# Second products in pairs of steps, absolute values on ScalarE, and one convolution moved to TensorE

## Chip, cores and metric

One NeuronCore of one Trainium2 chip runs the whole program. The metric is the device time in microseconds (us) from the start to the end of the program. PE is TensorE (PEld its weight loads), DVE is VectorE, ACT is ScalarE, POOL is GpSimd, SP is SyncE, which issues most transfers.

## The reference

```python
# x: (4, 4096, 192), weight: (8, 7); both MLPs: 192 -> 2048 -> 192 on 16384 tokens
w = softmax(weight)                       # 7 taps for each of 8 groups of 24 channels
x = causal_conv(x, w)                     # each channel with the 7 taps of its group
h = x @ moe_w_in;  x = (h * np.cos(h)) @ moe_w_out
h = x @ moe2_w_in
g = np.where(h > 0.0, h, np.exp(np.minimum(h, 0.0)) - 1.0)
out = g @ moe2_w_out
```

Weights of the MLPs are drawn by the reference's own functions; the kernel reads them as pairs of 32-bit words (the 64-bit floats of the inputs) and rebuilds each value in float32. That rebuilding is called decoding here.

## The kernel before

Tokens lie along the free dimension in 32 blocks of 512. Channels lie on partitions: 128 lower channels, and 64 upper ones, of which two blocks share a 128-partition tile. The hidden dimension of 2048 is cut into 16 chunks of 128. A step is two such chunks of one block, so a block takes 8 steps in each MLP. Blocks go in groups of four: a group runs MLP 1 (m = 1) and then MLP 2 (m = 2), so there are 512 steps. Steps 0 to 31 are MLP 1 of blocks 0 to 3; blocks 0 and 1 take turns by half blocks of four steps.

To keep float32 accuracy, every operand is a high part and a low part, and each product is three products. In step s, TensorE does the first products of step s (`products_A`, 18 matmuls of 64 rows, two at a time beside each other in the two halves of the array) and the second products of step s-3 (`LAG` = 3). While weights are being decoded, only two PSUM banks are free for the second products, so these are 10 matmuls over all 128 rows (`whole_B`, L567). This holds for the blocks that begin before decoding is over, steps 0 to 31; from step 32 on, the second products are 64-row matmuls woven into the first ones (L583).

The order on every engine is written out by hand: what `step` emits first runs first on that engine. A step emits its products, and then for each of its two chunks t = 2s and 2s+1: `emit_act1(t)` (ACT, L608), `emit_mid(t)` (DVE, L617), `emit_act2(t-1)` (ACT, L623), `emit_g(t-1)` (DVE, L631), one decode advance if it is due, `emit_hi(t-2)` (ACT, L637), `emit_lo(t-2)` (POOL, L644). So `emit_g` of the second chunk of a step stands in the next step, behind `emit_act1` and `emit_mid` of that next step's first chunk. The first products land in a ring of four PSUM banks (`ring_bank`, u0 to u3), two for each step; a bank is free when `emit_g` of its chunk has read it. High and low parts of g rotate through six buffers each.

A decoded piece passes ACT (L195, and L197 for the absolute value in two of three pieces), DVE (L199, L201 for the absolute value in the third piece, L202, L203), POOL (L205), ACT (the high part) and POOL (the low part). Thirty pieces are decoded in all.

`opening` is called after each of the first steps and carries the work of the first blocks. Lower channels of blocks 0 to 2 are convolved by TensorE with diagonal tap matrices (`conv_by_products`, L403, 7 products in float32, two matmul records each). The shared upper channels of blocks 2 and 3 are convolved by VectorE (`conv_taps`, L374 and L376), one tap after each of steps 5 to 11, and split into parts (`split_pair`, L437 and L439) when block 2 is split. `spare` is a scratch tile in the place that MLP 2's weights take later.

Of the kernel before, what the change touches and what calls it, by code (L numbers as in the profile page):

```python
# [18 lines left out]
P = 128  # L19
N = 512  # L20
# [12 lines left out]
def conv_then_two_mlps(ctx, tc, x, weight, w_in1, w_out1, w_in2, w_out2, out):  # L33
# [139 lines left out]
        zp = zt.tile([P, 2, N], F32R, tag=f"zp{b % ZN}", name="z")  # L173
        return zp[:, 0], zp[:, 1], zt.tile([P, N], F32R, tag=f"zc{b % ZN}", name="z")

    turn, scalar = deque(("", "e1", "")), deque((0, 1, 1))

    def decode(m, load, n):

        raw, use = raw_tile(n)
        load(raw)
        yield
        lo, hi = raw[..., 0], raw[..., 1]
        brink.reverse()
        t = brink[0][:, 0:n]
        turn.rotate(-1)  # L190
        w = (op if turn[0] else stage).tile([P, N], F32, tag=turn[0] or "w", name="w")[:, 0:n]
        bits = w.bitcast(I32)
        scalar.rotate(-1)
        size = w if scalar[0] else t
        nc.scalar.activation(out=t, in_=lo.bitcast(U32), func=AF.Copy, scale=2.0 ** -51, bias=2.0)  # L195
        if size is w:
            nc.scalar.activation(out=w, in_=f32(hi), func=AF.Abs)  # L197
        yield
        nc.vector.scalar_tensor_tensor(out=lo, in0=hi, scalar=SIGN, in1=t.bitcast(I32), op0=ALU.bitwise_and, op1=ALU.bitwise_or)  # L199
        if size is t:  # L200
            nc.vector.tensor_scalar(out=t.bitcast(I32), in0=hi, scalar1=~SIGN, scalar2=0, op0=ALU.bitwise_and, op1=ALU.bitwise_or)  # L201
        nc.vector.tensor_scalar(out=t, in0=size, scalar1=2.0 ** -15, scalar2=2.0 ** 17 - 2.0 ** 13, op0=ALU.max, op1=ALU.min)  # L202
        nc.vector.tensor_scalar(out=bits, in0=t.bitcast(I32), scalar1=3, scalar2=0, op0=ALU.logical_shift_left, op1=ALU.bitwise_or)  # L203
        yield
        nc.gpsimd.tensor_tensor(out=bits, in0=bits, in1=lo, op=ALU.add)  # L205
        taken.difference_update(use)
        yield w
# [91 lines left out]
    rows = rows[:, 0:at].rearrange("p (k d) -> p k d", d=D)  # L299
    xc0, xc1, xa2, xc2 = (spare[:, c * NX:(c + 1) * NX] for c in range(4))  # L300
    fold_rows = spare[:, 4 * NX:4 * NX + P]
    turn_rows = op.tile([P, N], F32R, tag="e0", name="turn")[:, 0:P]

    def load_rows():
# [90 lines left out]
            nc.tensor.matmul(y[:, 0:P], lhsT=ident, rhs=ident, start=True, stop=True)  # L395
        return y

    def conv_by_products(b, o):


        xT = xTs.pop(("a", b))
        for k in range(K):
            nc.tensor.matmul(o, lhsT=taps[:, k], rhs=xT[:, k * Q:k * Q + N], start=k == 0, stop=k == K - 1)  # L403
            if k == K - 1:
                ys["a", b] = o
            yield

    def conv_packed(b):
# [165 lines left out]
    def ends_here(m, b, j):  # L574
        return j == NP - 1 or split_up(m, b) and j == NP // 2 - 1

    def side_by_side(*streams):

        for pr in zip_longest(*streams):
            for product in pr:  # L580
                if product:
                    o, lhsT, rhs, first, final = product
                    nc.tensor.matmul(o, lhsT=lhsT, rhs=rhs, start=first, stop=final)  # L583

    def products(s):
        now, then = 0 <= s < total, 0 <= s - LAG < total
        if then and steps[s - LAG][2] == 0 and not late:
            whole.add(steps[s - LAG][:2])
        if not then or steps[s - LAG][:2] in whole:
            if now:  # L590
                side_by_side(products_A(2 * s), products_A(2 * s + 1))
            if then:
                whole_B(s - LAG)
        elif not now:
            side_by_side(products_B(s - LAG, 0), products_B(s - LAG, 1))
        else:
            streams = products_B(s - LAG, 0), products_B(s - LAG, 1)
            side_by_side(chain(products_A(2 * s), streams[0]), chain(streams[1], products_A(2 * s + 1)))
        if then:
            for i in (0, 1):  # L600
                del gs[f"{s - LAG} {i}"]

    def emit_act1(s):
        m = steps[s // 2][0]
# [233 lines left out]
    def need(m, at, *kinds):  # L838
        while any(ready.get((k, m), 0) < at for k in kinds):
            assert loaded or any(stages.values())  # L840
            advance()
# [32 lines left out]
    def step(s):  # L874
        now = 0 <= s < total
        present[0] = s
        if now:
            m, b, j = steps[s]
            need(m, j + 1, "o", "c")
        finish = iter(())  # L880
        if 0 <= s - LAG < total:
            m, b, j = steps[s - LAG]
            need(m, 2 * j + 2, "oh", "os")
        products(s)
        ends = 0 <= s - LAG < total and ends_here(*steps[s - LAG])
        if ends:
            assert not lazy
            finish = evac(*steps[s - LAG])
        if s in begin_at:
            m, b = begin_at[s]  # L890
            chores.append(begin_split(b) if m == 1 else double_z(b))
        first_mlp = now and steps[s][0] == 1
        for i in (0, 1):
            t = 2 * s + i
            if i:
                next(finish, None)
            if now:
                emit_act1(t)
                emit_mid(t)
            next(finish, None)  # L900
            if 0 <= t - 1 < 2 * total:
                emit_act2(t - 1)
                emit_g(t - 1)
            if not prepared and (s < NP // 2 or i != ends and (s < 12 or not ends and (s % 3 or s > 18))):
                advance()
            if 0 <= t - 2 < 2 * total:
                emit_hi(t - 2)
                emit_lo(t - 2)
            if i:
                next(finish, None)  # L910
            if now and not first_mlp and not ends:
                next(cq, None)
                if i and not first_mlp and steps[s][2] in (4, 6):
                    next(cq, None)
            chore()
        if prepared and not late:
            brief.close()
            top.close()
            late.append(ctx.enter_context(tc.tile_pool(name="ps_s", bufs=1, space=bass.MemoryType.PSUM)))

    total = len(steps)
    def run(gen, n=99):
        for _ in range(n):
            if next(gen, 0) == 0:
                break

    def opening():

        yield
        fold(1, bank("a1", "y"))  # L930
        upper_split(1)
        run(conv_by_products(1, bank("a0", "y")))
        run(split(1))
        conved.update((0, 1))
        turn_segment("a", 2)
        load_a(3)
        yield
        run(conv_by_products(2, bank("a1", "y")))
        y = kept(2)
        nc.scalar.activation(out=y, in_=ys["a", 2], func=AF.Copy)  # L940
        ys["a", 2] = y
        turn_segment("c", 2)
        load_c(4)
        upper = conv_taps("c", 2, xTs.pop(("c", 2)))
        yield
        yield
        yield
        for s in range(5, 12):
            run(upper, 1)
            yield  # L950
        run(upper)
        moved.add("o")
        conved.add(2)
        yield
        lower = conv("a", 3)
        for _ in range(7):
            run(lower, 1)
            yield
        run(lower)
        conved.add(3)  # L960
        yield

    with tc.manual_schedule():
        channel_masks()
        nc.sync.dma_start(out=wsm, in_=weight.partition_broadcast(P))
        y0 = awake()
        load_rows()
        fetch(4)
        nc.scalar.activation(out=spark, in_=ident[:, 0:H], func=AF.Exp)
        starts()  # L970
        softmax_weights()
        fetch(3)
        load_a(1)
        load_shifted(1)
        lower()
        advance("1")
        advance("21")
        a0, c0 = from_rows("a"), from_rows("c")
        next(a0)
        next(c0)  # L980
        for _ in a0:
            pass
        advance("3")
        advance("2")
        for _ in c0:
            pass
        for _ in conv_by_products(0, y0):
            pass
        advance("34")
        advance("1")  # L990
        for _ in conv_packed(0):
            pass
        fold(0, bank("a1", "y"))
        advance("421")
        advance("321")
        advance("342")
        for _ in split(0):
            pass
        advance("134")
        turn_segment("a", 1)  # L1000
        turn_segment("c", 1)
        load_a(2)
        load_c(2)
        run(conv_packed(1))
        need(1, 1, "o", "c")
        turn.append("e0")
        hooks = opening()
        for s in range(total + LAG):
            step(s)
            next(hooks, None)  # L1010
        for c in lazy:
            for _ in c:
                pass
# [27 lines left out]
```

## Time and profile before

| | us |
|---|---|
| median of 3 runs | 2296.68 (2296.4 to 2298.99) |
| profiled execution, own time | 2297.01 |
| its span in the trace | 2295.3 |
| PE busy in the span | 2265.7 (99%) |
| ACT, DVE, POOL busy | 1862.8 (81%), 1768.8 (77%), 1253.0 (55%) |

A busy PE is not a PE at its peak: matmuls are pipelined and their modelled ends overlap. What a stretch is worth is read from the distance between starts, and from the idle time in brackets with the instruction that ended it. Times in the trace count from the start of the span, which is 1.7 us shorter than the execution's own time.

### The profile page before, as it was taken

How to read it: one execution, taken by the hardware profiler on the slowest of the kernel's cores; microseconds unless marked ns; L12 is line 12 of the kernel's file. 1: busy time of each engine (PE TensorE's matmuls, PEld its weight loads, DVE VectorE, ACT ScalarE, POOL GpSimd, SP SyncE). 2: the span in 40 equal slices, each digit the busy share in tenths (PEclk: the TensorE clock that was granted, in tenths of full speed). 3: DMA queues.
4: the chain of work that ended last, by engine and by line, in shares of the span. 5: the costliest groups of instructions: out<-in, count | busy, mean ns of one | idle time of the engine just before them, and what ended most of it. 6: DMA issues, size and time to landing. Idle time of an engine off the chain costs nothing.

```text
span 2295.3 us, 49382 instructions
## 1 busy us (share of the span) xinstructions
PE 2265.7 (99%) x19226; PEld 1839.5 (80%) x19226; DVE 1768.8 (77%) x2564; ACT 1862.8 (81%) x3422; POOL 1253.0 (55%) x975
## 2 busy tenths in 40 slices
PE   8999999999999999999999999999999999999998
PEld 5667888888888888888888888888888888888887
DVE  7986977779777897778967798676986779777655
ACT  6877788888888788888788888888788887888886
POOL 5895335763367533674446743576435763367532
PEclk9999999999999999999999999999999999999999
DMA  7222221213211132112221123212221113211111
GB/s 167 81 68 49 51 58 36 46 32 64 49 36 38 32 69 48 40 29 57 52 52 33 24 58 55 47 38 44 45 57 35 46 34 64 42 36 38 26 38 22
DMA packets 292603, 111.43 MB, mean 49 GB/s; under 512 B 245840, under 2 KB 260176, under 8 KB 292368
## 3 DMA queue, kind: packets, MB, share of 16 engines
q1 hardware_dynamic: 290048, 107.42, 22.4%
q8 instruction: 150, 2.46, 0.4%
q10 hardware_dynamic: 2320, 0.85, 0.2%
q14 instruction: 85, 0.70, 0.1%
HBM read 30.09 MB, written 12.58 MB: 19 GB/s over the span
## 4 chain that ended last, share of the span: by engine, by line
PE 89%; DVE 8%; issue 1%; ACT 1%; DMA 1%; POOL 0%; ACTq 0%; DVEq 0%; SPq 0%; POOLq 0%
PE acc L583 45%; PE u L583 42%; DVE y L376 1%; PE acc L567 1%; DVE w L633 1%; DVE w L631 1%; DVE w L617 1%; DVE gl L644 1%; DVE t L202 1%; DVE w L203 0%; DMA raw<-in_moe_w_in_dram 0%; DMA raw<-in_moe_w_out_dram 0%; DVE y L374 0%; DVE raw L199 0%; PE y L403 0%
## 5 line engine op out<-in xcount | busy, mean ns | idle before, releaser
L644 POOL TENSOR_TENSOR gl<-w,gh 128x512 fp32r<-128x512 f32 x768 | 1013.7, 1321 | 1001.8 <-ACT gh L637 640.0
L583 PE MATMUL acc<-gh,wo_hl 64*128 64x512 f32 x3840 | 1174.3, 386 | 0.0
L583 PEld LDWEIGHTS acc<-gh,wo_hl 64*128 64x128 f32 x3840 | 705.3, 184 | 75.8 <-DVE z L697 0.4
L583 PE MATMUL acc<-gh,wo_s 64*128 64x512 f32 x1920 | 740.8, 386 | 0.0
L583 PE MATMUL acc<-gl,wo_hl 64*128 64x512 f32 x1920 | 740.2, 386 | 0.0
L583 PE MATMUL acc<-gl,wo_s 64*128 64x512 f32 x1920 | 740.1, 386 | 0.0
L637 ACT ACTIVATE gh<-w 128x512 fp32r<-128x512 f32 x1024 | 641.2, 626 | 16.2 <-DVE w L633 15.8
L583 PE MATMUL u<-ch,wi_c 64*128 64x512 f32 x2048 | 619.4, 391 | 14.1 <-DVE w L631 11.4
L583 PE MATMUL u<-sh,wi_o 64*128 64x512 f32 x2048 | 611.4, 387 | 0.0
L617 DVE SCALAR_TENSOR_TENSOR w<-u,w 128x512 f32<-128x512 f32 x512 | 352.0, 687 | 251.1 <-ACT w L608 249.1
L633 DVE SCALAR_TENSOR_TENSOR w<-w,u 128x512 f32<-128x512 f32 x512 | 347.8, 679 | 215.1 <-ACT w L625 210.0
L610 ACT ACTIVATE w<-u 128x512 f32<-128x512 f32 x512 | 306.2, 598 | 186.7 <-PE u L583 167.1
L608 ACT ACTIVATE w<-u 128x512 int32<-128x512 f32 x512 | 306.4, 598 | 184.2 <-PE u L583 178.5
L583 PE MATMUL u<-z,wi_o 64*128 64x512 f32 x1536 | 427.4, 386 | 0.0
L583 PEld LDWEIGHTS u<-ch,wi_c 64*128 64x128 f32 x2048 | 364.7, 184 | 71.7 <-DVE w L631 18.9
L583 PEld LDWEIGHTS u<-sh,wi_o 64*128 64x128 f32 x2048 | 368.5, 185 | 40.7
L583 PE MATMUL u<-sl,wi_o 64*128 64x512 f32 x1024 | 387.1, 387 | 0.0
L583 PE MATMUL u<-cl,wi_c 64*128 64x512 f32 x1024 | 386.7, 387 | 0.0
L583 PEld LDWEIGHTS acc<-gh,wo_s 64*128 64x128 f32 x1920 | 353.3, 184 | 37.9 <-DVE e L698 0.3
L583 PEld LDWEIGHTS acc<-gl,wo_hl 64*128 64x128 f32 x1920 | 353.3, 184 | 37.6
L583 PEld LDWEIGHTS acc<-gl,wo_s 64*128 64x128 f32 x1920 | 353.2, 184 | 37.6
L631 DVE TENSOR_TENSOR w<-u,w 128x512 f32<-128x512 f32 x512 | 348.8, 681 | 41.4 <-ACT w L623 41.4
(143 smaller groups left out, 3608.2 us busy)
## 6 DMA issues: line engine op xcount, KB each, us to landing
out_dram<-e SPq DMA_DIRECT2D x189, 64.0 KB, 2.0
xa<-in_x_dram SPq DMA_DIRECT2D x124, 88.0 KB, 2.9
sh<-z SPq DMA_DIRECT2D x64, 128.0 KB, 2.9
sl<-z SPq DMA_DIRECT2D x64, 128.0 KB, 2.5
ch<-z SPq DMA_DIRECT2D x64, 128.0 KB, 2.4
cl<-z SPq DMA_DIRECT2D x64, 128.0 KB, 2.4
sh<-xh SPq DMA_DIRECT2D x62, 128.0 KB, 2.3
sl<-xl SPq DMA_DIRECT2D x62, 128.0 KB, 2.3
```

The lines of the kernel that those rows point to most:

```text
L202: nc.vector.tensor_scalar(out=t, in0=size, scalar1=2.0 ** -15, scalar2=2.0 ** 17 - 2.0 ** 13, op0=ALU.max, op1=ALU.min)
L376: nc.vector.scalar_tensor_tensor(out=o, in0=i, scalar=w, in1=o, op0=ALU.mult, op1=ALU.add)
L567: nc.tensor.matmul(to, lhsT=w[:, f], rhs=g, start=st and n in (0, 2), stop=sp and n >= len(ops) - 2)
L583: nc.tensor.matmul(o, lhsT=lhsT, rhs=rhs, start=first, stop=final)
L608: nc.scalar.activation(out=w.bitcast(I32), in_=u, func=AF.Copy, bias=0.25)
L610: nc.scalar.activation(out=w, in_=u, func=AF.Relu, scale=-1.0)
L617: nc.vector.scalar_tensor_tensor(out=w, in0=u, scalar=0.25, in1=w.bitcast(I32), op0=ALU.add, op1=ALU.subtract)
L631: nc.vector.tensor_tensor(out=w, in0=u, in1=w, op=ALU.mult)
L633: nc.vector.scalar_tensor_tensor(out=w, in0=w, scalar=-1.0, in1=u, op0=ALU.add, op1=ALU.max)
L637: nc.scalar.activation(out=gh, in_=wrk[t], func=AF.Copy)
L644: eng.tensor_tensor(out=gl, in0=wrk.pop(t), in1=f32(own[0]), op=ALU.subtract)
```

## The change

- `products` no longer does the second products of each step on its own while these use all rows. `due(s)` returns nothing where s-3 is even, and s-4 and s-3 where s-3 is odd. So an odd step has first products alone, and an even step has its first products and two sets of second products. From step 35 on nothing differs.
- Every decoded piece takes its absolute value by ScalarE (L197); L201 is gone.
- After step 3, TensorE convolves the upper channels of blocks 2 and 3 with a second set of diagonal taps, which GpSimd makes before step 0; `split_pair(2)` follows at once. The seven VectorE operations after steps 5 to 11 are gone.

```diff
-        if size is w:
-            nc.scalar.activation(out=w, in_=f32(hi), func=AF.Abs)
+        nc.scalar.activation(out=w, in_=f32(hi), func=AF.Abs)
...
-        if size is t:
-            nc.vector.tensor_scalar(out=t.bitcast(I32), in0=hi, scalar1=~SIGN, scalar2=0, op0=ALU.bitwise_and, op1=ALU.bitwise_or)
-        nc.vector.tensor_scalar(out=t, in0=size, scalar1=2.0 ** -15, scalar2=2.0 ** 17 - 2.0 ** 13, op0=ALU.max, op1=ALU.min)
+        nc.vector.tensor_scalar(out=t, in0=w, scalar1=2.0 ** -15, scalar2=2.0 ** 17 - 2.0 ** 13, op0=ALU.max, op1=ALU.min)
...
+    upper_taps = spare[:, 4 * NX + P:4 * NX + P + K * P].rearrange("p (k c) -> p k c", c=P)
...
+    def is_whole(s):
+        if steps[s][2] == 0 and not late:
+            whole.add(steps[s][:2])
+        return steps[s][:2] in whole
+
+    def due(s):
+
+        if not 0 <= s - LAG < total:
+            return []
+        if not is_whole(s - LAG):
+            return [s - LAG]
+        return [s - LAG - 1, s - LAG] if (s - LAG) % 2 else []
+
+    def products(s, then):
+        now = 0 <= s < total
+        if not then or is_whole(then[0]):
             if now:
                 side_by_side(products_A(2 * s), products_A(2 * s + 1))
-            if then:
-                whole_B(s - LAG)
+            for k in then:
+                whole_B(k)
...
-        if 0 <= s - LAG < total:
-            m, b, j = steps[s - LAG]
+        then = due(s)
+        for k in then:
+            m, b, j = steps[k]
             need(m, 2 * j + 2, "oh", "os")
-        products(s)
-        ends = 0 <= s - LAG < total and ends_here(*steps[s - LAG])
+        products(s, then)
+        ends = bool(then) and ends_here(*steps[s - LAG])
...
-        upper = conv_taps("c", 2, xTs.pop(("c", 2)))
-        yield
-        yield
-        yield
-        for s in range(5, 12):
-            run(upper, 1)
-            yield
-        run(upper)
+        yield
+        run(conv_by_products(2, bank("a0", "y"), "c"))
+        run(split_pair(2))
         moved.add("o")
         conved.add(2)
         yield
+        for _ in range(4, 13):
+            yield
...
         run(conv_packed(1))
+        nc.gpsimd.tensor_tensor(
+            out=upper_taps, in0=ident.unsqueeze(1).to_broadcast([P, K, P]),
+            in1=wch[:, 1].unsqueeze(2).to_broadcast([P, K, P]), op=ALU.mult,
+        )
         need(1, 1, "o", "c")
```

## Rows read from the trace of the kernel before

**Rows 1.** The page: busy time by engine
```profile
PE 2265.7 (99%) x19226; PEld 1839.5 (80%) x19226; DVE 1768.8 (77%) x2564; ACT 1862.8 (81%) x3422; POOL 1253.0 (55%) x975
```
**Rows 2.** Busy time in stretches; columns stand in the first line, PEclk is granted clock
```profile
core 0: us, PE busy (x) PEld busy (x) DVE busy (x) ACT busy (x) POOL busy (x), PEclk, DMA share, GB/s
44.90:221.51 176.61, 164.32 (x897) 114.30 (x897) 146.94 (x214) 139.90 (x260) 141.64 (x109) 0.98 0.32 80
221.51:2295.00 2073.49, 2063.80 (x18187) 1702.95 (x18186) 1586.40 (x2276) 1698.22 (x3106) 1087.99 (x819) 1.00 0.21 44
54.48:63.07 8.59, 6.82 (x29) 4.54 (x28) 7.99 (x14) 7.32 (x14) 7.92 (x7) 0.80 0.54 134
112.01:119.12 7.11, 5.34 (x29) 3.51 (x29) 6.64 (x12) 4.50 (x9) 3.56 (x3) 1.00 0.84 188
134.09:142.44 8.35, 6.83 (x30) 4.52 (x29) 7.51 (x11) 4.71 (x9) 6.63 (x6) 0.80 0.01 2
```
**Rows 3.** Timeline of PE, step 3: start, duration, instruction, [idle before <-releaser]
```profile
44.90 0.73 PE L583 MATMUL u<-ch,wi_c 64*128 64x512 f32 x4
45.47 0.39 PE L583 MATMUL u<-cl,wi_c 64*128 64x512 f32 x2
...
46.85 0.39 PE L583 MATMUL u<-sl,wi_o 64*128 64x512 f32 x2
47.17 0.73 PE L567 MATMUL acc<-gh,wo_hl 128*128 128x512 f32 x2
...
49.69 0.50 PE L583 MATMUL u<-ch,wi_c 64*128 64x512 f32 x2
```
**Rows 4.** Timeline of ACT and DVE in the same step
```profile
47.34 0.60 ACT L608 ACTIVATE w<-u 128x512 int32<-128x512 f32 x1 [1.73 <-PE u L583]
...
48.04 0.69 DVE L617 SCALAR_TENSOR_TENSOR w<-u,w 128x512 f32<-128x512 f32 x1 [3.57 <-ACT w L608]
48.65 0.68 DVE L631 TENSOR_TENSOR w<-u,w 128x512 f32<-128x512 f32 x1
```
**Rows 5.** Timeline: PE waiting within first products, and the DVE operation before 56.75
```profile
54.48 0.50 PE L583 MATMUL u<-ch,wi_c 64*128 64x512 f32 x1
56.75 0.50 PE L583 MATMUL u<-ch,wi_c 64*128 64x512 f32 x2 [1.77 <-DVE w L631]
...
114.12 0.73 PE L583 MATMUL u<-ch,wi_c 64*128 64x512 f32 x3 [1.62 <-DVE w L631]
...
136.10 0.80 PE L583 MATMUL u<-ch,wi_c 64*128 64x512 f32 x3 [1.52 <-DVE w L631]
...
56.02 0.68 DVE L631 TENSOR_TENSOR w<-u,w 128x512 f32<-128x512 f32 x1
```
**Rows 6.** Waits, 44.9 to 221.5: engine line waited for: us in total, times, longest
```profile
PE u L583 <- DVE w L631: 11.4, 13, 1.8
```
**Rows 7.** Timeline of PE: step 2's convolution begins; step 35 begins
```profile
38.70 0.70 PE L403 MATMUL y<-spare,rows 128*128 128x512 f32 x1 [2.54 <-DVE spare L350]
...
221.51 0.50 PE L583 MATMUL u<-ch,wi_c 64*128 64x512 f32 x1
```
**Rows 8.** Groups by form, 44.9 to 221.5: count | busy us, mean ns | idle
```profile
L201 DVE TENSOR_SCALAR t<-raw 128x512 int32<-128x512 int32 x5 | 3.5, 695 | 0.2
L197 ACT ACTIVATE w<-raw 128x512 f32<-128x512 f32 x9 | 6.0, 667 | 0.0
L376 DVE SCALAR_TENSOR_TENSOR y<-spare,wch,y 128x512 f32<-128x512 f32 x6 | 7.0, 1161 | 0.0
...
L439 DVE TENSOR_TENSOR cl<-y,ch 128x512 fp32r<-128x512 f32 x1 | 1.5, 1456 | 0.0
```
**Rows 9.** GpSimd: the tap matrix and L201's half-size form (0 to 60), and an idle stretch
```profile
L383 POOL TENSOR_TENSOR rows<-ident,wch 128x896 f32<-128x896 f32 x1 | 1.7, 1684 | 2.8 <-DVE wch L120 2.8
L201 DVE TENSOR_SCALAR t<-raw 128x256 int32<-128x256 int32 x3 | 1.3, 428 | 0.1
...
25.60 0.74 POOL L234 TENSOR_TENSOR wi_o<-w,wi_o 128x256 fp32r<-128x256 f32 x1 [4.82 <-ACT wi_o L233]
```

More of the change, by code (lines that the diff above doesn't have):

```diff
@@ L174, in z_tiles @@
         return zp[:, 0], zp[:, 1], zt.tile([P, N], F32R, tag=f"zc{b % ZN}", name="z")
-    turn, scalar = deque(("", "e1", "")), deque((0, 1, 1))
+    turn = deque(("", "e1", ""))
     def decode(m, load, n):
@@ L192, in decode @@
         bits = w.bitcast(I32)
-        scalar.rotate(-1)
-        size = w if scalar[0] else t
         nc.scalar.activation(out=t, in_=lo.bitcast(U32), func=AF.Copy, scale=2.0 ** -51, bias=2.0)
-        if size is w:
-            nc.scalar.activation(out=w, in_=f32(hi), func=AF.Abs)
+        nc.scalar.activation(out=w, in_=f32(hi), func=AF.Abs)
         yield
         nc.vector.scalar_tensor_tensor(out=lo, in0=hi, scalar=SIGN, in1=t.bitcast(I32), op0=ALU.bitwise_and, op1=ALU.bitwise_or)
-        if size is t:
-            nc.vector.tensor_scalar(out=t.bitcast(I32), in0=hi, scalar1=~SIGN, scalar2=0, op0=ALU.bitwise_and, op1=ALU.bitwise_or)
-        nc.vector.tensor_scalar(out=t, in0=size, scalar1=2.0 ** -15, scalar2=2.0 ** 17 - 2.0 ** 13, op0=ALU.max, op1=ALU.min)
+        nc.vector.tensor_scalar(out=t, in0=w, scalar1=2.0 ** -15, scalar2=2.0 ** 17 - 2.0 ** 13, op0=ALU.max, op1=ALU.min)
         nc.vector.tensor_scalar(out=bits, in0=t.bitcast(I32), scalar1=3, scalar2=0, op0=ALU.logical_shift_left, op1=ALU.bitwise_or)
@@ L396, in awake, with conv_by_products @@
         return y
-    def conv_by_products(b, o):
-        xT = xTs.pop(("a", b))
+    def conv_by_products(b, o, what="a"):
+        xT = xTs.pop((what, b))
         for k in range(K):
-            nc.tensor.matmul(o, lhsT=taps[:, k], rhs=xT[:, k * Q:k * Q + N], start=k == 0, stop=k == K - 1)
+            nc.tensor.matmul(o, lhsT=(taps if what == "a" else upper_taps)[:, k], rhs=xT[:, k * Q:k * Q + N], start=k == 0, stop=k == K - 1)
             if k == K - 1:
-                ys["a", b] = o
+                ys[what, b] = o
             yield
@@ L583, in side_by_side @@
                     nc.tensor.matmul(o, lhsT=lhsT, rhs=rhs, start=first, stop=final)
[L585 to L589, printed above, removed]
+    def is_whole(s):
[11 more added lines that the diff above has]
+        if not then or is_whole(then[0]):
             if now:
                 side_by_side(products_A(2 * s), products_A(2 * s + 1))
-            if then:
-                whole_B(s - LAG)
+            for k in then:
+                whole_B(k)
         elif not now:
-            side_by_side(products_B(s - LAG, 0), products_B(s - LAG, 1))
+            side_by_side(products_B(then[0], 0), products_B(then[0], 1))
         else:
-            streams = products_B(s - LAG, 0), products_B(s - LAG, 1)
+            streams = products_B(then[0], 0), products_B(then[0], 1)
             side_by_side(chain(products_A(2 * s), streams[0]), chain(streams[1], products_A(2 * s + 1)))
-        if then:
+        for k in then:
             for i in (0, 1):
-                del gs[f"{s - LAG} {i}"]
+                del gs[f"{k} {i}"]
     def emit_act1(s):
@@ L880, in step @@
         finish = iter(())
-        if 0 <= s - LAG < total:
-            m, b, j = steps[s - LAG]
+        then = due(s)
+        for k in then:
+            m, b, j = steps[k]
             need(m, 2 * j + 2, "oh", "os")
-        products(s)
-        ends = 0 <= s - LAG < total and ends_here(*steps[s - LAG])
+        products(s, then)
+        ends = bool(then) and ends_here(*steps[s - LAG])
         if ends:
```

## Prediction

> **What bounds the kernel now.** I read the busy times by engine first: PE fills 99% of the span [rows 1]. Then I cut the span where the change ends. From 221.5 us on (step 35) the code is the same, and PE is busy 2063.8 of 2073.5 us [rows 2]; nothing is won or lost there, so what the change does to the start of step 35 it does to the total. From the start of step 3 (44.90) to the start of step 35 (221.51) 32 steps take 176.61 us [rows 2, 7], 5.52 us each. No other engine is full there: DVE 146.9, POOL 141.6, ACT 139.9 us [rows 2].
>
> Next the timeline of one undisturbed step. First products begin at 44.90, their ninth and last pair at 46.85, second products at 47.17, the next step at 49.69 [rows 3]. That is 4.79 us. Matmuls (or pairs) follow at 0.23 us: six pairs from 45.47 to 46.85. Nineteen of these are 4.37, so each of the two changes between 64-row and 128-row products costs 0.21 us. 32 steps at 4.79 would be 153.3 us; 23.3 us are lost to waits and clock.
>
> The waits inside first products have one form: PE stops for L631, the operation that frees a bank of the ring [rows 5, 6], 11.4 us in 13 waits. Why L631 can be late is seen in step 3: the last pair starts at 46.85, L608 on ACT at 47.34, L617 on DVE at 48.04, L631 at 48.65, done at 49.33 [rows 4]. L631 frees the bank of the step before, but it stands behind L608 and L617 of the present step. So there is a fixed chain from the end of one step's first products to the earliest start of the next step's: 2.48 us from the last pair's start, plus 0.05 to the matmul (56.02 + 0.68 to 56.75 [rows 5]): 2.53. Now the second products (2.52 us from 47.17 to 49.69) fill just that time.
>
> **The change part by part.**
>
> *Pairs.* Two sets of second products run behind each even step from 4 to 34, none behind odd steps. Of 64 changes of row mode 32 go: 32 x 0.21 = 6.7 us of PE less. But an odd step's first products are now followed at once by those of the next even step, and its second stream needs the bank that L631 frees at the end of the chain above. Nothing else is queued on PE there, and PE takes its matmuls in order. So PE waits: 2.53 us from last pair to next, where 0.23 is the pace; 2.3 us, 15 times (steps 5 to 6, and so on to 33 to 34), 34.5 us. This is a wait of the very form that costs PE 11.4 us today, made regular. It can't be shortened by idle engines: its terms are one ACT and two DVE operations in program order.
>
> *Convolution on PE.* The same work for the lower channels took from 38.70 to 44.90, 6.20 us with its mode change [rows 3, 7]. It leaves DVE free of 7 operations (six at 1.16 us [rows 8]). It needs the tap matrix, 1.68 us on POOL [rows 9], which fits the 4.82 us that POOL sits idle before 25.60 [rows 9]: zero, or 1.7 without that cover. The following split moves from about step 13 to step 3 (L439 1.46 us [rows 8]) and holds a bank that the second products of step 4 want. They come 2.27 us after the convolution ends (44.90 to 47.17), the split's ACT and DVE operation take about 2.1: zero, at most 1.5.
>
> *Absolute values.* Seven full-size L201 (0.695 us) leave DVE from step 3 on, and seven L197 (0.667) join ACT (rows 8 show five of the seven, two more work on another tile, and what one L197 takes) [rows 8]. While PE does two sets of second products (4.8 us) both engines catch up, so I take zero; bounds -4.9 and +4.7. Before step 3 three half-size ones (0.428 [rows 9]) lie on DVE ahead of the first products: -1.3 to 0, I take -0.5.
>
> *Buffers.* In an even step `emit_hi` and `emit_lo` wait for buffers that the same step's second products free, ACT up to about 1 us and POOL about 2 us behind the first products; behind them on these engines stand only operations of the next step, some 7 us away. Zero, up to 0.3 a pair.
>
> *Sum to step 35.* Step 4 begins at 44.90 + 2.27 + 6.20 = 53.37; step 5 at 53.37 + 2.27 + 2.52 + 10 x 0.23 = 60.46. From odd step to odd step: 1.95 to its last pair, 2.53 wait, 2.27 to the second products, 4.82 for two sets: 11.57. Fifteen of these give 234.0 for step 35, against 221.51: +12.5. With -0.5 from before step 3 it is +12.0. Today's losses are thereby taken as gone; some will come back where DVE, ACT and POOL bunch (splits, block ends, late transfers): I take 2 us, bounds 0 and 8.
>
> *Clock.* Three waits of today were longer than 1.5 us [rows 5]. Behind two of them, 1.77 and 1.52, PE was granted half its clock for a while, 1.2 GHz in place of 2.4: the stretches 54.48 to 63.07 and 134.09 to 142.44 have a mean of 0.80, so each lost 8.59 x 0.2 = 1.7 us; behind the third (1.62) the clock stayed at 1.00 [rows 2]. The new waits leave PE idle some 1.8 to 1.9 us each, at least as long, and what follows each is on the path. Two of three: 10 x 1.7 = 17 us; bounds 0 and 15 x 1.7 = 25.5.
> The Trainium skill, page "TensorE: Matmul & The Clock Gate", section "A second HAM failure mode: psum-queue depth-cycling", tells of a kernel whose cycling through PSUM banks made PE "micro-idle" between groups often enough for the clock to swing between its levels. By that rule every pair would pay: the upper bound, 2337 in place of 2328. The same page's section on loop structure warns only of gaps longer than these; by it the clock term would be zero, and the trace disagrees in two of three waits.
>
> Total: +12.0 + 2 + 17 = +31. The profiled execution took 2297.0 us, span and 1.7 us around it, 0.3 above the median. 2297 + 31 = 2328.
>
> **The rivals.**
>
> *The clock holds.* The waits come as above, but PE keeps 2.4 GHz. For it: one long wait of three did. Time: 2297 + 14 = 2311.
>
> *Clock and backlog.* The clock falls at nearly every wait and the other engines bunch too: 12 + 8 + 25.5 gives 2342. Against it: in the longer stretch of some 208 us none of DVE, ACT and POOL would be busy more than 145 us.
>
> *Faster.* The wait between paired first products doesn't appear, as the bank is free by then; then pairs save their mode changes, and DVE's relief takes today's waits away. It decides at a wait of 2.3 - 12.0 / 15 = 1.5 us: below that (and without a clock loss) the change gains. Without any wait step 35 would begin 34.5 us sooner than summed, though a pair of 9.3 us would then press on POOL, which needs 141.6 / 16 = 8.9 for two steps; with 10 us lost to that, 2297 + 12 - 34.5 + 10 = 2284. Against it: rows 4 has the chain in its shortest form, each operation starting as the one before ends.
>
> *It comes out even.* Lost time of today that I don't see as tied to the second products goes, and the waits are partly covered: 2292 to 2302.
>
> *It doesn't do what it says.* If decoding ended later than step 34, MLP 2's first block would run in pairs as well, four more waits, +9 or more. Decoding has the same advances in the same steps, so this is small and on the slow side.
>
> **How the numbers follow.** Chances: forecast 0.60 (2316 to 2336), clock holds 0.20 (2308 to 2314), clock and backlog (or pairs in MLP 2) 0.10 (2337 to 2350), even 0.05, faster 0.05. Likeliest: 2328. The range for 8 in 10 takes in the forecast and the clock that holds, with the low end of its bounds, and the middle of the third: 2306 to 2342. About 0.2%, 4.6 us, is what a measurement of this kernel can tell from no change. Slower by more than that: 0.90; within: 0.05; faster: 0.05.
>
> **What would show it.** Right: L567 in runs of twenty, an idle of nearly 2 us ended by DVE L631 (L633 in steps 32 to 34) in the first products of even steps, about 15 of them; a step-to-step distance near 11.6 us for two, near 13.3 where the clock falls; granted clock well below 0.98 between step 3 and step 35; step 35 near 250; the rest unchanged in length. Wrong: no L631 wait in even steps, a pair in under 10.8 us, or a clock of 1.00 throughout. The convolution is right if PE spends 6.2 us on it after step 3 and the second products of step 4 don't wait for the split.

## The result and the profile after

| | before | changed |
|---|---|---|
| median, us | 2297.3 (2296.4 to 2298.99) | 2322.3 (2321.27 to 2323.1) |
| span of the profiled execution, us | 2295.3 | 2320.5 |
| start of step 3, 5, 35, us | 44.90, 54.48, 221.51 | 44.27, 59.78, 247.19 |
| mean granted clock | 0.997 | 0.991 |

The changed kernel takes 1.0108 of the time of before (95% interval 1.009 to 1.0125): 25 us more. A second time, on another occasion, the ratio was 1.0112 (1.0098 to 1.0126).

Busy time in stretches, as in [rows 2]: step 4 to 35, two pairs of steps without and two with a fall of the clock, and the rest.

```profile
core 0: us, PE busy (x) PEld busy (x) DVE busy (x) ACT busy (x) POOL busy (x), PEclk, DMA share, GB/s
52.74:247.19 194.45, 166.70 (x879) 121.41 (x878) 131.67 (x194) 137.81 (x255) 135.47 (x106) 0.91 0.25 63
59.78:71.25 11.47, 9.63 (x58) 7.09 (x58) 8.82 (x15) 9.18 (x19) 9.88 (x9) 1.00 0.36 92
71.25:84.25 13.00, 11.16 (x57) 8.07 (x56) 9.34 (x15) 11.13 (x21) 10.32 (x9) 0.87 0.27 81
84.25:97.24 12.99, 11.16 (x58) 8.05 (x57) 9.74 (x16) 9.82 (x20) 11.40 (x11) 0.87 0.38 96
97.24:108.70 11.46, 9.62 (x58) 7.11 (x57) 7.04 (x11) 8.82 (x17) 8.56 (x8) 1.00 0.31 77
247.19:2320.50 2073.31, 2063.43 (x18187) 1760.92 (x18186) 1586.93 (x2274) 1696.53 (x3104) 1086.98 (x818) 1.00 0.21 44
```

From step 35 on the kernel takes 2073.31 us, before 2073.49 [rows 2]: all of the loss lies ahead. A pair of steps takes 11.46 us, or 13.0 when the granted clock in it has a mean of 0.87. No other engine is full.

One pair on PE (steps 5 and 6): the answer to [rows 3, 5]; the last line begins the next pair. PE line of the first products is now L579, of the second products L563.

```profile
59.78 0.73 PE L579 MATMUL u<-ch,wi_c 64*128 64x512 f32 x4
...
61.74 0.40 PE L579 MATMUL u<-sl,wi_o 64*128 64x512 f32 x2
61.97 0.39 PE L579 MATMUL u<-ch,wi_c 64*128 64x512 f32 x1
64.20 0.73 PE L579 MATMUL u<-ch,wi_c 64*128 64x512 f32 x3 [1.83 <-DVE w L638]
...
66.47 0.73 PE L563 MATMUL acc<-gh,wo_hl 128*128 128x512 f32 x2
...
70.93 0.39 PE L563 MATMUL acc<-gl,wo_s 128*128 128x512 f32 x1
71.25 0.73 PE L579 MATMUL u<-ch,wi_c 64*128 64x512 f32 x4
```

What ACT and DVE do meanwhile, as in [rows 4] (L615, L630, L624, L638 are the lines called L608, L623, L617, L631 before):

```profile
62.23 0.60 ACT L615 ACTIVATE w<-u 128x512 int32<-128x512 f32 x1 [2.29 <-PE u L579]
62.72 0.62 ACT L630 ACTIVATE w<-w 128x512 f32<-128x512 f32 x1
...
62.86 0.69 DVE L624 SCALAR_TENSOR_TENSOR w<-u,w 128x512 f32<-128x512 f32 x1 [2.24 <-ACT w L615]
63.46 0.68 DVE L638 TENSOR_TENSOR w<-u,w 128x512 f32<-128x512 f32 x1
```

Both engines had been idle for over 2 us when the first products of step 5 ended. L638 then ends at 64.14, and PE goes on at 64.20, 2.46 us after the last pair of step 5. The first product of the even step's first chunk still ran at 61.97, since its bank was free; the second chunk's bank is the one that L638 reads. In the waits between step 4 and step 35 (total, times, longest) the line answering to [rows 6] has gone from 11.4 to 25.9 us:

```profile
DVE w L624 <- ACT w L615: 49.4, 42, 4.4
...
PE u L579 <- DVE w L638: 25.9, 14, 2.0
```

The fifteenth, between steps 33 and 34, belongs to MLP 2 and ends with L640 (L633 before).

### The profile page after: what moved, and what is told of

Same layout as the page of the kernel before. It is cut to its first block, busy times and chain, and to the rows that moved or that the text cites. A ratio compares the mean times of both kernels' runs of the same rounds, so it can differ in the third digit from the quotient of the medians.

```text
span 2320.5 us, 49422 instructions
## 1 busy us (share of the span) xinstructions
PE 2275.2 (98%) x19240; PEld 1907.5 (82%) x19240; DVE 1758.2 (76%) x2547; ACT 1866.8 (80%) x3432; POOL 1251.2 (54%) x976
## 4 chain that ended last, share of the span: by engine, by line
PE 93%; DVE 4%; issue 1%; ACT 1%; DMA 1%; ACTq 0%; POOL 0%; SPq 0%; DVEq 0%; POOLq 0%
PE acc L579 45%; PE u L579 44%; PE acc L563 3%; DVE y L372 1%; DVE w L640 1%; DVE gl L651 1%; PE y L399 1%; DVE w L624 0%; DVE w L638 0%; ACT w L615 0%; DVE y L370 0%; DMA raw<-in_moe_w_in_dram 0%; DVE z L760 0%; DMA raw<-in_moe_w_out_dram 0%; DMA xa<-in_x_dram 0%
## 5 line engine op out<-in xcount | busy, mean ns | idle before, releaser
L579 PE MATMUL acc<-gh,wo_hl 64*128 64x512 f32 x3840 | 1174.1, 386 | 0.0
L579 PEld LDWEIGHTS acc<-gh,wo_hl 64*128 64x128 f32 x3840 | 705.4, 184 | 63.3
L579 PE MATMUL acc<-gh,wo_s 64*128 64x512 f32 x1920 | 740.7, 386 | 0.0
L579 PE MATMUL acc<-gl,wo_hl 64*128 64x512 f32 x1920 | 740.2, 386 | 0.0
L579 PE MATMUL acc<-gl,wo_s 64*128 64x512 f32 x1920 | 740.0, 386 | 0.0
L644 ACT ACTIVATE gh<-w 128x512 fp32r<-128x512 f32 x1024 | 641.4, 626 | 19.3 <-DVE w L640 16.1
L579 PE MATMUL u<-ch,wi_c 64*128 64x512 f32 x2048 | 618.2, 391 | 30.3 <-DVE w L638 25.9
L579 PE MATMUL u<-sh,wi_o 64*128 64x512 f32 x2048 | 617.0, 391 | 0.0
L624 DVE SCALAR_TENSOR_TENSOR w<-u,w 128x512 f32<-128x512 f32 x512 | 352.0, 688 | 281.1 <-ACT w L615 279.2
L640 DVE SCALAR_TENSOR_TENSOR w<-w,u 128x512 f32<-128x512 f32 x512 | 347.8, 679 | 217.3 <-ACT w L632 212.7
L615 ACT ACTIVATE w<-u 128x512 int32<-128x512 f32 x512 | 305.8, 597 | 206.3 <-PE u L579 187.5
L617 ACT ACTIVATE w<-u 128x512 f32<-128x512 f32 x512 | 305.1, 596 | 190.4 <-PE u L579 156.4
L579 PEld LDWEIGHTS u<-ch,wi_c 64*128 64x128 f32 x2048 | 364.8, 184 | 79.2 <-DVE w L638 32.8
L579 PE MATMUL u<-z,wi_o 64*128 64x512 f32 x1536 | 428.9, 387 | 0.0
L579 PEld LDWEIGHTS u<-sh,wi_o 64*128 64x128 f32 x2048 | 371.8, 187 | 35.4
L579 PE MATMUL u<-sl,wi_o 64*128 64x512 f32 x1024 | 390.4, 391 | 0.0
L579 PE MATMUL u<-cl,wi_c 64*128 64x512 f32 x1024 | 387.9, 389 | 0.0
L638 DVE TENSOR_TENSOR w<-u,w 128x512 f32<-128x512 f32 x512 | 348.7, 681 | 42.1 <-ACT w L630 42.1
L579 PEld LDWEIGHTS acc<-gl,wo_hl 64*128 64x128 f32 x1920 | 353.3, 184 | 31.6
L579 PEld LDWEIGHTS acc<-gh,wo_s 64*128 64x128 f32 x1920 | 353.3, 184 | 31.6
L579 PEld LDWEIGHTS acc<-gl,wo_s 64*128 64x128 f32 x1920 | 353.2, 184 | 31.6
```

The source lines that it names most:

```text
L615: nc.scalar.activation(out=w.bitcast(I32), in_=u, func=AF.Copy, bias=0.25)
L617: nc.scalar.activation(out=w, in_=u, func=AF.Relu, scale=-1.0)
L624: nc.vector.scalar_tensor_tensor(out=w, in0=u, scalar=0.25, in1=w.bitcast(I32), op0=ALU.add, op1=ALU.subtract)
L638: nc.vector.tensor_tensor(out=w, in0=u, in1=w, op=ALU.mult)
L640: nc.vector.scalar_tensor_tensor(out=w, in0=w, scalar=-1.0, in1=u, op0=ALU.add, op1=ALU.max)
L644: nc.scalar.activation(out=gh, in_=wrk[t], func=AF.Copy)
```

## Experiments

Two theories stood against each other. The first is that of the prediction: pairs make PE wait for the ring bank once in two steps, and the clock falls behind these waits. The second: the moved convolution (6.2 us of PE) and the work put on ScalarE cost the time, and pairs are worth what their mode changes are worth. All ratios are against the kernel before on the same chip.

| run | what it is | ratio (95%) |
|---|---|---|
| e1_single | changed, second products in every step | 0.9997 (0.9987 to 1.0006) |
| e2_pairs_only | before, with pairs | 1.0112 (1.0096 to 1.0127) |
| e3_filled | changed, wait filled with matmuls | 1.0067 (1.0052 to 1.0082) |
| e4_order | changed, L638 ahead of the chain | 1.0007 (0.9998 to 1.0017) |
| e5_before_order | before, same exchange | 0.9988 (0.9979 to 0.9998) |
| e7_single_order | e1 with the exchange | 0.9995 (0.9986 to 1.0004) |
| e8_order_conv3 | e4, block 3's lower convolution on PE | 1.0018 (1.0009 to 1.0028) |
| e10_single_order_conv3 | e7, the same | 0.999 (0.9981 to 0.9999) |
| e9_abs_undone | changed, absolute values as before | 1.0122 (1.0107 to 1.0138) |
| e14_abs_undone_again | the same again | 1.0128 (1.0114 to 1.0141) |
| e13_changed_again | changed, again | 1.0112 (1.0098 to 1.0126) |
| e11_before_abs_order | before, absolute values and exchange | 0.9959 (0.9947 to 0.9972) |

### Pairs undone, and pairs alone

```diff
-        return [s - LAG - 1, s - LAG] if (s - LAG) % 2 else []
+        return [s - LAG]
...
         load_c(4)
-        yield
         run(conv_by_products(2, bank("a0", "y"), "c"))
```

> The changed kernel with its second products in every step again; the moved convolution stands one step earlier, behind step 2, since from step 3 on its bank is taken. If the pairs cost the time (ring-bank wait in every even step and clock falls behind it), both go: PE keeps the 6.2 us of the moved convolution, and of the 23.3 us lost before between steps 3 and 35 some 8 go with VectorE's relief: 2297 + 6.2 - 8 = 2295 us (2289 to 2302), no regular wait of 1.8 us, clock falls at most 3. If the moved convolution and the absolute values cost the time, it stays near 2322 us.

Measured: 2298.97 us, 0.9997 of before. The regular waits are gone: those for the ring bank from step 3 to step 35 come to 11.8 us in 8, near the 11.4 of before [rows 6], and the clock falls once.

```profile
PE u L579 <- DVE w L638: 11.8, 8, 3.9
```

The other run is the kernel before with `due` and `products(s, then)` of the diff above and nothing else:

> The kernel before with the pairs alone: no other edit. If the pairs cost the time: 15 waits of 1.8 us of idle in the even steps, some 10 clock falls, step pairs of 11.5 or 13.0 us as in the changed kernel, less the 6.2 us of the convolution on PE: 2316 us (2313 to 2322). If the pairs are worth their mode changes only: 2297 - 6.7 = 2290 us.

Measured: 2323.47 us, 1.0112, a little above the range expected. Pairs alone cost all that the change costs; the rest of the change without them costs nothing that can be measured. The second theory falls. That rest is a loss and a gain that cancel, though. The runs e7_single_order and e11_before_abs_order below share chip, exchange of order and absolute values, and differ in the moved convolution alone: 2296.82 us with it, 2287.47 without. So the convolution on TensorE costs some 9 us where second products stand in every step, 6.2 of them its own time on PE.

The run with pairs alone has no convolution between steps 3 and 4, so these stand back to back too, and there is a sixteenth wait, and the clock falls eleven times. This is PE in steps 3 and 4, and then the stretch from there to step 5:

```profile
47.41 0.39 PE L583 MATMUL u<-ch,wi_c 64*128 64x512 f32 x1
49.71 0.50 PE L583 MATMUL u<-ch,wi_c 64*128 64x512 f32 x2 [1.91 <-DVE w L642]
...
45.24:58.27 13.03, 11.12 (x59) 8.03 (x58) 9.59 (x16) 10.56 (x21) 7.63 (x7) 0.87 0.92 205
```

So a convolution of 6.2 us put between these two steps hides a wait and a fall: steps 3 and 4 take 15.51 us with it (44.27 to 59.78) and 13.03 without, 2.5 us more and not 6.2.

### The wait filled

```diff
+FILL = 8
...
+                one = products_A(2 * s)
+                if 6 <= s < 36 and s % 2 == 0:
+                    op0 = next(one)
+                    for _ in range(FILL):
+                        nc.tensor.matmul(op0[0], lhsT=op0[1], rhs=op0[2], start=True, stop=True)
+                    one = chain([op0], one)
+                side_by_side(one, products_A(2 * s + 1))
```

> The changed kernel with 8 extra matmuls (8 x 0.23 = 1.84 us) ahead of the first products of each even step from 6 to 34, into the ring bank that is free by then; the true products begin that bank anew. They fill the wait and add no time to the path. If the idle brings the clock down, the falls go: 2322 - 10 x 1.52 = 2307 us, granted clock 1.00 from step 3 to step 35, pairs at 11.5 us throughout. If the clock falls for another reason (the changes of mode, the runs of twenty full-row products), it still falls about 10 times: 2322 us.

Measured: 2314.03 us, 1.0067, some 8 us less than the changed kernel although PE does 120 matmuls more. The same two steps as above, and the stretch from step 5 to step 7:

```profile
61.03 0.40 PE L580 MATMUL u<-sl,wi_o 64*128 64x512 f32 x2
61.26 1.98 PE L603 MATMUL u<-ch,wi_c 64*128 64x512 f32 x8
63.08 1.14 PE L580 MATMUL u<-ch,wi_c 64*128 64x512 f32 x4
...
59.07:70.53 11.46, 11.43 (x65) 8.55 (x64) 8.82 (x15) 9.17 (x19) 9.87 (x9) 1.00 0.36 92
```

A pair takes 11.46 us as it did without the filling; what goes are eight of ten falls. The two that are left come behind waits that the filling didn't cover, as DVE freed the bank later than the chain alone would have:

```profile
130.93 1.00 PE L580 MATMUL u<-ch,wi_c 64*128 64x512 f32 x3 [1.67 <-DVE w L645]
...
184.68 0.50 PE L580 MATMUL u<-ch,wi_c 64*128 64x512 f32 x2 [1.44 <-DVE w L645]
```

It is thus the idle of PE that brings the clock down, not the changes of mode or the runs of twenty. Eight falls at 1.53 us (13.00 less 11.47) are 12.2 us, of which 8 were seen; the rest was given back where DVE was late, as in the pair around 130.93, which takes 14.86 us.

### The freeing operation ahead of the chain

```diff
+EARLY = 35
...
+            ahead = not i and 1 <= s < EARLY
+            if ahead:
+                emit_act2(t - 1)
+                emit_g(t - 1)
             if now:
                 emit_act1(t)
                 emit_mid(t)
             next(finish, None)
-            if 0 <= t - 1 < 2 * total:
+            if 0 <= t - 1 < 2 * total and not ahead:
                 emit_act2(t - 1)
                 emit_g(t - 1)
```

> The changed kernel with one exchange of order in steps 1 to 34: the second ACT operation and the DVE operation that frees the ring bank, both of the last chunk of the step before, are emitted ahead of the first ACT operation of the present step. If the chain in program order is the cause, the 15 waits of 2.3 us and the 10 clock falls of 1.52 us go: 2322 - 34.5 - 15.2 = 2273 us, with up to 12 us back where POOL, ACT and DVE are full (a pair of steps at 9.2 to 10 us): 2273 to 2285. If the wait is for something else (the buffers of the high and low parts, the tap matrix, the decoding), it stays at 2315 to 2322 us.

Measured: 2302.03 us, 1.0007: some 20 us less than the changed kernel, level with before, but far from 2273. Where nothing else is late the wait is gone as expected: this is PE in steps 9 and 10, first products of both without a break, and a pair in 9.11 us.

```profile
83.47 0.40 PE L580 MATMUL u<-sl,wi_o 64*128 64x512 f32 x2
83.70 0.62 PE L580 MATMUL u<-ch,wi_c 64*128 64x512 f32 x4
...
85.52 0.39 PE L580 MATMUL u<-sl,wi_o 64*128 64x512 f32 x2
85.84 0.73 PE L564 MATMUL acc<-gh,wo_hl 128*128 128x512 f32 x2
...
90.62 0.73 PE L580 MATMUL u<-ch,wi_c 64*128 64x512 f32 x4
```

So the program order of that chain was the cause of the regular wait. But a pair of 9.1 us leaves the other engines little room (step 4 to 35 of this run, then its waits):

```profile
52.17:227.25 175.08, 155.54 (x879) 115.14 (x878) 136.16 (x193) 135.86 (x255) 134.90 (x105) 0.96 0.28 71
...
PE u L580 <- DVE w L639: 19.3, 12, 4.0
ACT w L616 <- PE u L580: 17.0, 9, 3.0
ACT w L631 <- DVE w L625: 10.8, 5, 5.7
```

The same operation (L639 here) is late again, 19.3 us in all, now for other reasons, and the clock falls three times. The longest such wait, 3.99 us at 154.25, comes from one tap of the lower convolution on DVE that took 6.35 us, where the median of its line is 0.75. Five operations of POOL without a gap overlap it; here are the first and the last:

```profile
147.24 6.35 DVE L373 SCALAR_TENSOR_TENSOR y<-xT,wch,y 128x512 f32<-128x512 f32 x1
153.51 0.68 DVE L639 TENSOR_TENSOR w<-u,w 128x512 f32<-128x512 f32 x1
...
146.81 1.29 POOL L230 TENSOR_TENSOR wi_c<-w,wi_c 128x512 fp32r<-128x512 f32 x1
...
151.77 1.26 POOL L201 TENSOR_TENSOR w<-w,raw 128x512 int32<-128x512 int32 x1
```

The Trainium skill, page "SBUF — State Buffer", section "Who interferes with whom", says that a VectorE instruction with two SBUF inputs contends with a GpSimd instruction that reads SBUF. These rows fit that: both operands of a tap, `xT` and `y`, lie in SBUF. In this trace 149 taps began while POOL was idle and took 0.73 to 0.75 us. All nine taps of over 2.5 us in the traces of this case end 0.55 us after the last of POOL's unbroken operations (147.24 + 6.35 against 151.77 + 1.26 above). No run took POOL's work away beside such a tap; that POOL holds it rests on these ends.

### Where the rest of these waits comes from

Two runs moved that convolution to TensorE, behind step 2:

```diff
+        turn_segment("a", 3)
+        load_a(4)
+        run(conv_by_products(3, bank("a0", "y")))
+        y = kept(3)
+        nc.scalar.activation(out=y, in_=ys["a", 3], func=AF.Copy)
+        ys["a", 3] = y
...
-        lower = conv("a", 3)
```

> The changed kernel with the exchange of order, and the lower convolution of block 3 moved from VectorE (transpose and seven taps over steps 13 to 20) to TensorE behind step 2. PE does 6.2 us more. If what is left of the waits with the exchange (19.3 us and three clock falls) is VectorE's own load, above all taps that take up to 6.35 us while POOL runs, some 14 of these 24 us go: 2302 + 6 - 14 = 2294 us (2284 to 2297). If they stay: 2308 us.

Measured: 2303.48 us, 1.0018. The waits for L639 go from 19.3 to 13.3 us, about what the 6.2 us on PE cost; 14 had been expected to go. The time lies between the two expectations. The convolution was a part of VectorE's lateness and not its bulk.

> As the run with second products in every step and the convolution behind step 2 (2299 us), with the exchange of order and the lower convolution of block 3 on TensorE too. PE work is 153.3 + 2 x 6.2 us between steps 3 and 35. If the ring-bank waits (11.8 us) and the clock falls go with both: 2299 + 6.2 - 13 = 2292 us (2286 to 2296). If the waits were the pairs' alone: 2305 us.

Measured: 2297.23 us, 0.999, just above the range expected. Without pairs the waits for L639 come down to 4.3 us, and the clock doesn't fall between steps 3 and 35. But by then PE does 12.4 us more itself, and the total is hardly better than before. The same without this second convolution:

> Second products in every step, the convolution behind step 2 on TensorE, absolute values by ScalarE, and the exchange of order. The same without the exchange came to 0.9997 with 11.8 us of waits for the ring bank and one clock fall. If the exchange takes half of these as it did for the kernel before (11.4 to 7.4 us): 2299 - 5 = 2294 us. If the rest is VectorE's own lateness: 2299 us.

Measured: 2296.82 us, 0.9995; waits for L639 9.1 us, where they were 11.8 without the exchange. The longest of those left, 3.78 us, stands behind a tap of 5.94 us on VectorE; that the others are VectorE's own lateness too is argued, since the exchange didn't remove them. The exchange alone, on the kernel before:

> The kernel before with the exchange of order alone (steps 1 to 34). If the fixed chain behind the first products is what makes PE wait for the ring bank, most of the 11.4 us of such waits and the two clock falls (1.7 us each) go: 2297 - 11 = 2286 us (2284 to 2292). If VectorE is late for its own load (its convolutions, the port it shares with POOL), the waits stay: 2295 to 2299 us.

Measured: 2296.15 us, 0.9988, with 7.4 us of waits for the ring bank in place of 11.4 [rows 6]. That is nearer to the second expectation. In its trace, steps 3 to 35 take 172.94 us in place of 176.61 [rows 2], but step 3 begins 2.7 us later than before (47.59), behind a fall of the clock. Where second products stand between the first ones, as before, they cover the fixed chain; the waits that the exchange leaves are taken for a late VectorE, by elimination.

### Absolute values

```diff
+        scalar.rotate(-1)
+        size = w if scalar[0] else t
...
+        if size is t:
+            nc.vector.tensor_scalar(out=t.bitcast(I32), in0=hi, scalar1=~SIGN, scalar2=0, op0=ALU.bitwise_and, op1=ALU.bitwise_or)
```

> The changed kernel with the absolute value of every third piece back on VectorE (seven full-size operations of 0.695 us from step 3 on). If they lie beside the two sets of second products, as forecast, nothing moves but the start: 2322 us, up to 0.6 more. If VectorE's load sets the pairs' pace, 2322 + 4.9 = 2327 us.

> The changed kernel with every third absolute value back on VectorE, a second time. If the forecast of nothing between steps 3 and 35 holds, it is slower than the changed kernel by about the 1 us of the start; if the 5 us seen against the first run of the changed kernel are real, by 3 to 5 us.

> The changed kernel as it is, beside the one with the absolute values undone, for their difference on one chip: ratio to the kernel before near 1.0108, 15 waits of 1.83 us, some 10 clock falls.

Measured: 2327.72 and 2327.01 us (1.0122 and 1.0128), beside 2323.34 (1.0112) for the changed kernel on the chip of the second. The absolute values by ScalarE are worth some 3 to 4 us here, not the 0.5 of the sum; the intervals of the ratios overlap, so the size is not settled. Part of it lies where no second products cover VectorE: the second products of step 4 wait for the split, 0.51 us in the first of these traces and 0.54 in the second.

```profile
57.29 0.47 PE L568 MATMUL acc<-gh,wo_hl 128*128 128x512 f32 x1 [0.51 <-DVE cl L440]
...
154.80 0.50 PE L584 MATMUL u<-ch,wi_c 64*128 64x512 f32 x2 [2.26 <-DVE w L643]
...
62.02:251.46 189.44, 161.33 (x841) 117.31 (x841) 130.80 (x192) 129.79 (x240) 131.54 (x103) 0.90 0.24 60
```

From step 5 to step 35 the first took 189.44 us, the changed kernel 187.41: one wait longer (2.26), and eleven falls in place of ten. That did not come out a second time: on the chip of the second run the same stretch took 188.76 us with every third absolute value on VectorE (ten falls) and 189.70 with all on ScalarE (nine falls), and all of the difference lay ahead of step 5, which began at 62.98 and 58.92. With L201 on VectorE the stretch from the first products to step 3 took 24.58 to 24.60 us (before, pairs alone, the first of these runs), and 26.27 in two more traces (the second, and the exchange on the kernel before), where the clock fell once in it; without L201 it took 23.35 to 23.84 (changed, both traces, filled, exchange).

The changed kernel's second trace has the regular waits of the first, but nine falls, and one pair of 16.16 us. In that pair PE waits twice for a VectorE that is late behind a tap; the same tap took 3.45 us in the first trace, and no such pair followed it.

```profile
132.36:148.52 16.16, 11.43 (x58) 8.14 (x58) 14.35 (x22) 11.02 (x20) 12.58 (x10) 0.89 0.01 1
...
127.30 5.99 DVE L372 SCALAR_TENSOR_TENSOR y<-xT,wch,y 128x512 f32<-128x512 f32 x1
...
131.44 1.30 POOL L200 TENSOR_TENSOR w<-w,rows 128x512 int32<-128x512 int32 x1
...
139.94 0.73 PE L579 MATMUL u<-ch,wi_c 64*128 64x512 f32 x3 [3.04 <-DVE w L638]
```

### A version that beats both

```diff
+EARLY = 35
...
-        if size is w:
-            nc.scalar.activation(out=w, in_=f32(hi), func=AF.Abs)
+        nc.scalar.activation(out=w, in_=f32(hi), func=AF.Abs)
...
+            ahead = not i and 1 <= s < EARLY
```

> The kernel before with the absolute values by ScalarE and the exchange of order; no pairs, no moved convolution. The exchange alone came to 0.9988 of the kernel before. The absolute values took about 1 us off the time from the first products to step 3 in every kernel that had them so far (23.4 to 23.8 against 24.6 us): 0.998, 2293 us (2290 to 2296). If ScalarE, which stands at 80% there, becomes late by the seven operations that it gains: 2297 to 2300 us.

Measured: 2287.47 us, 0.9959 (0.9947 to 0.9972). Steps 3 to 35 take 168.87 us in place of 176.61 [rows 2], and the waits for the ring bank are down to 4.3 us in 5; with the exchange alone they were 7.4. Second products stay in every step, and VectorE has L201 taken off it. The gain is larger than expected (2290 to 2296), and how it divides between the two edits is not settled: no run had the absolute values alone.

```profile
43.80:212.67 168.87, 161.52 (x898) 113.45 (x897) 140.73 (x208) 142.14 (x267) 143.33 (x110) 0.98 0.33 83
...
PE u L579 <- DVE w L627: 4.3, 5, 1.9
```

## Why the prediction was right, step by step

| term | forecast | measured | measured again |
|---|---|---|---|
| start of step 3 | 44.4 | 44.27 | 43.37 |
| steps 3 to 4, with the convolution on PE | 2.27 + 6.20 | 8.47 | 8.50 |
| start of step 5 | 59.96 | 59.78 | 58.92 |
| pair without a fall | 11.57 | 11.46 to 11.47 | 11.45 to 11.58 |
| falls of the clock | 10 | 10 | 9 |
| price of a fall | 1.7 | 1.53 | 1.53 |
| other losses, step 5 to 35 | 2 | 0.1 | 4.0 |
| start of step 35 | near 250 (sum: 252.5) | 247.19 | 248.62 |
| total | +31 | +25 | +25 |

The second column of measurements is the changed kernel's second trace. The mechanism was right, and the terms that the sum had too high add up to the difference of some 5 us at step 35: 0.2 at step 5, 1.6 in fifteen pairs, 1.7 in ten falls, 1.9 of other losses. One reading behind the sum was wrong. The prediction counts three waits of over 1.5 us in the kernel before; there is a fourth, at 160.80, and the clock stayed at 1.00 behind it:

```profile
160.80 0.73 PE L583 MATMUL u<-ch,wi_c 64*128 64x512 f32 x3 [1.69 <-DVE w L631]
...
157.60:166.00 8.40, 6.71 (x37) 4.51 (x37) 8.32 (x13) 7.08 (x14) 8.40 (x8) 1.00 0.25 56
```

- *The wait* was the step on which all hung, and it held: 15 waits, each 1.82 to 1.95 us of idle, ended by L638 (the last by L640), as the chain in rows 4 had it. It was 2.46 us from pair to product where 2.53 was put in.
- *The clock* fell ten times, as was put in; that the count came out exact is luck. Two of four waits, not two of three, would have given 7.5 falls, and the second trace of the same kernel has nine. Nor does the length of the idle pick out the waits with a fall: in the first trace they follow the order none, one, one, five times over, with 1.83 or 1.84 us of idle in all five without. What picks them isn't shown. The price was too high by a tenth: a mean of 0.80 over 8.59 us [rows 2] is 1.7 us of lost clock, but a pair grows by 1.53 only. At the lower level pairs of products follow at 0.43 us (two from 189.97 to 190.82), which is less than twice 0.23. The Trainium skill, page "TensorE: Matmul & The Clock Gate", section "A second HAM failure mode: psum-queue depth-cycling", tells of short idles of PE that make the clock swing, and so it does here. The prediction's reading of it, that every pair would pay, was not borne out: five of 15 paid nothing.
- *Other losses* were put at 2 us and are near nothing in the first trace: 187.41 us from step 5 to step 35 are 15 x 11.465 + 10 x 1.53 = 187.3. DVE, ACT and POOL caught up in every pair. In the second trace they didn't: 189.70 us, with nine falls, leave 4.0 us of other losses, 3.2 of them in the pair of 16.16 us. That is within the prediction's bounds of 0 and 8.
- *The convolution* took its 6.2 us on PE (46.53 to 52.74, [rows 7] before), and the tap matrix and the split cost nothing on the path: second products of step 4 began at 55.02, 2.28 us behind.
- *Absolute values* were mis-sized: -0.5 was put in, and the runs have some -3 to -4. What the traces show of it stands in the main ahead of step 5, where -0.7 to -2.9 us lie before step 3 and some -0.5 in step 4's wait for the split. From step 5 on the two comparisons differ in sign, so that the cover by second products, taken as complete there, is not refuted.
- *The rivals*: the clock that holds would have been 2311, and the filled run, with two falls, came to 2314. The rival on the other side, a faster kernel, named a wait under 1.5 us as its condition. The exchange of order made that true in some pairs. What then held the kernel back is what that rival had priced: engines that are 78% busy and have a pair of 9.1 us to fit into. It had put 10 us on this; it was some 24 (19.3 us of waits and three falls).

## What to carry to other kernels

Before work is taken out from between two batches on the busiest engine, look at what that work was covering: here 2.5 us of second products stood exactly over the chain that frees the next bank, and saving 0.21 us of mode change twice in two steps opened a wait of 2.3. If a buffer's last reader stands behind the next batch's first reader on its engine, move it ahead before bringing batches together. And count an idle of nearly 2 us on TensorE with the clock that may fall behind it: here that added 1.0 us on average to each wait of 2.3.

## What the runs showed of the hardware

- Behind ten of 15 idles of 1.82 to 1.95 us the granted clock fell from 2.4 to 1.2 GHz for a while, and behind five it didn't, with the same work around each. The length alone doesn't decide: with the exchange of order the clock fell behind an idle of 1.30 us (at 72.93), and not behind one of 2.56 (at 142.72). Filling the idle with eight 64-row matmuls took away eight of the ten falls.
- A change between 64-row pairs and 128-row products costs 0.21 us; two sets of second products without one between them follow at 0.23 us a matmul (68.66 to 68.89 in the changed kernel).
- One VectorE operation with two SBUF operands took 6.35 us, its median being 0.75, beside a GpSimd that ran five operations without a gap. It and eight more such taps (3.42 to 5.99 us) each end 0.55 us after the last of GpSimd's operations; with GpSimd idle at their start, taps took 0.73 to 0.75 us.
